# Later conversion stages, another PSUM buffer for one state part, and a new order of one projection in a linear-attention and feed-forward kernel

## The chip, the core and the metric

The kernel runs on one core of one Trainium2 chip. The metric is the device time of one execution in microseconds (us). Five engines work side by side, each through its own instructions in order: TensorE (PE, matrix products; the loading of its weights is shown apart as PEld), VectorE (DVE), ScalarE (ACT), GpSimd (POOL) and SyncE (SP, which here only issues transfers). They wait for each other through semaphores.

## What is computed

The reference has two parts. The first is a linear attention with decay, over 4 batches, 8 heads, 768 tokens and a head dimension of 48:

```python
for t in range(S):
    cur = np.einsum('bhd,bhe->bhde', u[None] * kt, vt)
    y[:, :, t] = np.einsum('bhd,bhde->bhe', rt, state + cur)
    state = wt[:, :, :, None] * state + np.einsum('bhd,bhe->bhde', kt, vt)
```

Its output, with the heads put side by side, is x: 3072 tokens by 384. The second part is a feed-forward layer with 2048 hidden columns:

```python
h = x @ w_in
sp = np.maximum(h, 0.0) + np.log1p(np.exp(-np.abs(h)))
g = h * erf(sp)
return (g @ w_out).astype(np.float32)
```

The arrays w_in and w_out are given as 64-bit floats; the kernel turns them into 32-bit floats itself, by operations on their words.

## The kernel before

**Steps.** The work is cut into twelve steps, s = 0 to 11. A step handles 128 tokens of two batches and all their heads. The code counts from zero, and so does this text: the change's title calls s = 1 "step two" and s = 2 "step three".

**The attention of a step** (`attend`, for s = 0 to 4) goes through six levels. A level makes products of r and k with each other on PE (`level_products`, L436) in a PSUM buffer `pp`; `scale` (L252, VectorE) multiplies r and k by decays for the next level, in place, so it must wait until PE has read them; `take_level` copies the masked products into `own` (L448 on VectorE for levels two to five, two copies of L455 on ScalarE for level six; level one is L651). Then PE multiplies `own` by v (L470, `from_own`, in two calls), transposes k (L663, copied to `kT` by ScalarE at L667), and makes the state part (L522, `state_part`), which VectorE adds to the state (L690 or L692, then L693 on GpSimd, then L695). Last, `through_state` (L496) adds what the old state gives; ScalarE copies the result to xT (L503 to L506), and six small transfers (L510), three issued by SP and three by ScalarE, move the rest of it into place.

**The two `pp` buffers.** `products` hands out the PSUM buffers pp0 and pp1 in turn. While the weights are being converted it always gives pp0, and pp1 belongs to the conversion. Whoever writes such a buffer waits until its last content has been read.

**The feed-forward of a step** runs later, in pieces between the attention's products. `hidden` (L731) multiplies xT by w_in: of step s - 1, a piece being two tiles of 128 hidden columns, six matmuls, and a copy to h on ScalarE (L740). There are sixteen such tiles in two groups g of eight. Softplus (L713), erf (L716) and the product with h (L720, VectorE) follow group by group. `project` (L754) multiplies the result by w_out: of step s - 3, in pieces of four matmuls, group by group and in a group first all eight tiles for output j = 0 and then for j = 1; the output is copied at L763 and stored. In step 1 the pieces are those of step 0's hidden layer, one at each place; in step 3 the first projection runs.

**The conversion of the weights** (`convert`) is cut into sixteen chunks of two tiles, 0 to 7 for w_in and 8 to 15 for w_out. A chunk has three stages: `load` (L194, 768 KB, issued by SP, three buffers), `scale` (two operations on ScalarE: L207 into pp1, L209 into `rest`) and `join` (VectorE: L216 on pp1 and L219 from pp1 to the weights; GpSimd: the add L223). Since pp1 is one buffer, a chunk's L207 waits for the L219 of the chunk before. A load waits for the L219 that frees its buffer.

**What sets the order.** All five engines take their instructions in the order in which the program writes them. `place(n)` is called after level n + 1 and at the ends of a step; in steps 0 to 3 it sends the letters of the table CONVERT (L811) to the conversion, `l`, `s` and `j` for the three stages, and then a piece of the feed-forward follows. In steps 1 and 2 the letters go ahead of the softplus and erf stages. Entry n of a row belongs to place n; entry 8 is sent behind the step's `through_state`. So chunk k's stages stand at fixed places: in step 1, place 0 joins chunk 2 and scales chunk 3, between L651 and the scaling for level two, and place 4 joins chunk 6 and scales chunk 7, ahead of level six. Piece k of step 1 reads chunk k.

Of the kernel before, what the change touches and what calls it, by code (L numbers as in the profile page):

```python
# [11 lines left out]
FP32 = mybir.dt.float32  # L12
# [3 lines left out]
ALU = mybir.AluOpType  # L16

P = 128
EP = 64
HC = 64  # L20
NC = 2
NJ = 2
FG = 8
# [18 lines left out]
LOG = 6  # L42
# [18 lines left out]
def kernel(  # L61
# [14 lines left out]
    nc = tc.nc  # L76
    PSUM = bass.MemoryType.PSUM

    n_steps, _, _, JP, C = rkw.shape
# [45 lines left out]

    turns = {"next": 0, "converting": False}

    def products(shape):


        n = 0 if turns["converting"] else turns["next"]
        turns["next"] = 1 - n
        return ps_p.tile(shape, FP32, name=f"pp{n}")
# [46 lines left out]
    def convert(weights):  # L180

        held = {}

        def load(i):
            if i >= len(weights):
                return
            dst, src = weights[i]
            if src.dtype == FP32:  # L190
                nc.sync.dma_start(out=dst, in_=src)
                return
            words = wide.tile([P, 2, DM, 2], I32, name="words", bufs=3)
            nc.sync.dma_start(  # L194
                out=words[:].rearrange("p i n two -> p i (n two)"), in_=src.bitcast(I32)
            )
            held[i] = [words]

        def scale(i):
            if i in held:  # L200
                words = held[i][0]
                low, high = words[:, :, :, 0], words[:, :, :, 1]
                base = ps_p.tile([P, 2, NP * C], FP32, name="pp1")[:, :, :DM]
                rest = wide.tile([P, 2, DM], I32, name="rest", bufs=2)


                nc.scalar.mul(out=base, in_=high.bitcast(FP32), mul=2.0**-112)  # L207

                nc.scalar.mul(out=rest[:], in_=low.bitcast(U32), mul=2.0**-29)  # L209
                held[i] += [base.bitcast(I32), rest]  # L210

        def join(i):
            if i in held:
                words, bits, rest = held.pop(i)
                into = weights[i][0].bitcast(I32)
                nc.vector.tensor_scalar(  # L216
                    out=bits, in0=bits, scalar1=3, scalar2=None, op0=ALU.logical_shift_left
                )
                nc.vector.scalar_tensor_tensor(  # L219
                    out=into, in0=words[:, :, :, 1], scalar=-(1 << 31), in1=bits,  # L220
                    op0=ALU.bitwise_and, op1=ALU.bitwise_or,
                )
                nc.gpsimd.tensor_tensor(out=into, in0=into, in1=rest[:], op=ALU.add)  # L223

        done = {"l": 0, "s": 0, "j": 0}
        for _ in range(3):
            load(done["l"])
            done["l"] += 1
        while True:
            what = yield  # L230
            {"l": load, "s": scale, "j": join}[what](done[what])
            done[what] += 1
            if weights[0][1].dtype != FP32:
                turns["converting"] = 0 < done["s"] and done["j"] < len(weights)
                turns["next"] = 0

    def rows(e, n=D):
# [372 lines left out]
    def attend(s, xT, place, behind):  # L610

        c, in_t, vt, made, S, S_next, ends = parts_of(s)
        K = in_t[:, 1]
        RK = in_t[:, 0:2]


        following = prepare(s + 1) if s + 1 < n_steps else iter(())
        own = made if s >= DIRECT else att.tile([P, NH, HC], FP32, name="own")

        def keep_busy(*columns):  # L620
            zeros = states[1][0][:].rearrange("p n d -> p (n d)")
            for n in columns if not s else ():
                nc.tensor.matmul(
                    y[:].rearrange("p e j q t -> p (e j q t)")[:, :n], lhsT=ident[:],
                    rhs=zeros[:, :n], start=True, stop=True, skip_group_check=True,
                )

        def stay_warm(times=1, where=None):
            for _ in range(times):
                ps = where or ps_m.tile([P, NP * C], FP32, name="m")  # L630
                nc.tensor.matmul(
                    ps[:], lhsT=ident[:], rhs=ws[s][:, :NP], start=True, stop=True
                )

        if s == DIRECT:
            next(following)
        for level in range(near_log(s) + 1 if s == DIRECT else 1, LOG + 1):
            rk = made[:] if level == 1 else RK
            pp = products([P, NE, JP, HC])
            level_products(pp, rk, level)  # L640
            if level == LOG and s == DIRECT:
                spread_blocks(s + 1, pp)
            scale(s, level)
            keep_busy(DM, DM // 2)
            if level == 1 and s == 1:
                stay_warm()
            got = pp[:].rearrange("p e n t -> p (e n) t")
            if level == 1:
                if not s:
                    nc.vector.tensor_copy(out=first[:], in_=mask_sb[:, 0, :])  # L650
                nc.vector.tensor_mul(  # L651
                    own[:], got, first[:, None, :].to_broadcast([P, NH, HC])
                )
            else:
                take_level(own, pp, level)
            if level > 1 and (s, level) != (DIRECT, LOG - 1):
                next(following, None)
            place(level - 1)

        from_own(s, own, 1)  # L660
        ps = products([P, JP, P])
        for n in range(JP):
            nc.tensor.transpose(ps[:, n, :], K[:, n, :], ident[:])  # L663
        if not s:
            stay_warm()
        kT = att.tile([P, NH, D], FP32, name="kT", bufs=1)
        nc.scalar.copy(  # L667
            kT[:].rearrange("p (e n) d -> p e n d", e=NE),
            ps[:].rearrange("p n (e d) -> p e n d", e=NE)[..., :D],
        )  # L670
        if c:
            nc.gpsimd.tensor_mul(
                faded[0][:], S[:], ends[:, :, 0:1].to_broadcast([P, JP, D])
            )
        next(following, None)
        place(LOG)


        if s:
            ps = products([P, NC, JP, HC])  # L680
            ps = [ps[:, h] for h in range(NC)]
        else:
            ps = [ps_m.tile([P, JP, HC], FP32, name="m") for h in range(NC)]
        state_part(s, kT, ps)
        from_own(s, own, 0)
        if not s:
            stay_warm(1, products([P, NP * C]))
        for e in range(NE):
            if c:
                nc.vector.tensor_add(middle[rows(e)], faded[0][rows(e)], ps[0][rows(e), :, :D])  # L690
            else:
                nc.vector.tensor_copy(middle[rows(e)], ps[0][rows(e), :, :D])  # L692
        nc.gpsimd.tensor_mul(faded[1][:], middle[:], ends[:, :, 1:2].to_broadcast([P, JP, D]))  # L693
        for e in range(NE):
            nc.vector.tensor_add(S_next[rows(e)], faded[1][rows(e)], ps[1][rows(e), :, :D])  # L695
        for _ in following:
            pass
        place(LOG + 1)
        through_state(s, xT)
        behind()  # L700
# [44 lines left out]
    def project(s, gs):  # L745

        c, i = divmod(s, SPC)
        ps = [None] * NJ
        for g in range(NG):
            for j in range(NJ):  # L750
                if not g:
                    ps[j] = ps_m.tile([P, DM], FP32, name="m")
                for f in range(FG):
                    nc.tensor.matmul(  # L754
                        ps[j][:],
                        lhsT=gs[g][:, f, j * C : (j + 1) * C],
                        rhs=w_out_sb[:, g * FG + f, :],
                        start=g + f == 0,
                        stop=g == NG - 1 and f == FG - 1,
                    )  # L760
                    if g == NG - 1 and f == FG - 1:
                        o = outs.tile([P, DM], FP32, name="o")
                        nc.scalar.copy(o[:], ps[j][:])  # L763
                        nc.sync.dma_start(out=out[i * NJ + j, c], in_=o[:])
                    if f % 4 == 3:
                        yield
# [29 lines left out]
    def in_order(s, k):  # L796
# [13 lines left out]

    CONVERT = (  # L811
        ("", "", "", "", "", "s", "jls", "j", "sl"),
        ("jsl", "jsl", "jsl", "jsl", "jsl", "j", "", "", "sl"),
        ("jsl", "jsl", "jsl", "jsl", "jsl", "js"),
        ("js", "j"),
    )

    STAGES = {
        1: (0, 0, 0, 0, 0, 0, 1, 0), 2: (1, 0, 0, 0, 0, 0, 1, 1), 3: (1, 2, 1, 0, 0, 2, 1, 1)
# [8 lines left out]
    with tc.manual_schedule(  # L828
# [20 lines left out]
        for s in range(n_steps):  # L849
# [31 lines left out]
            if s > DIRECT:  # L881
                attend_late(s, place)
                continue
            attend(s, xTs[s], place, lambda: convert_at(LOG + 2))
            if s + 2 < n_steps:
                load_step(s + 2)
                if s + 2 == DIRECT:
# [107 lines left out]
```

## Time and profile before

| what | value |
| --- | --- |
| median of 9 runs | 619.95 us (619.19 to 621.9) |
| the profiled execution | 620.11 us |
| its span in the profile | 618.3 us |
| PE busy | 604.4 us |
| DVE, ACT, POOL busy | 412.4, 293.5, 291.7 us |
| PE busy between 104.8 and 130.0 us | 25.20 us |
| stretch in which the steps 1 and 2 lie | about 32 to 104 us |

The profile is one execution recorded by the hardware. A line of its timeline has the start, the duration, the engine, the line of the kernel, the operation, the tiles (result, arrow, operands), their shapes and the number of instructions that were merged, and in brackets how long the engine had been idle ahead of it and what ended that. An idle engine costs time only if somebody on the chain that ends last waits for it. A wait for several semaphores is put down to the one that the profile saw last, so the name in the brackets can be that of another.

### The profile page before, as it was taken

To read this page: it belongs to the slowest core of one execution; us is meant where nothing else is said; L and a number is where in the kernel's file an instruction comes from. 1 tells how busy PE (TensorE), PEld (TensorE's weight loads), DVE (VectorE), ACT (ScalarE), POOL (GpSimd) and SP (SyncE) were. 2 spreads that over 40 slices of the span, in tenths; PEclk is the share of its full clock that TensorE was granted. 3 is DMA by queue.
4 is the path that set the end of the run, shared out by engine and by line. 5 is a ranking of instruction groups with operands and counts; after the bars stand their busy time and mean duration, and the time that the engine had idled before them with its cause. 6 is when DMAs were issued, how large, how long until landed. Compare 5 with 4: busy or idle time off the path is not lost.

```text
span 618.3 us, 15587 instructions
## 1 busy us (share of the span) xinstructions
PE 604.4 (98%) x6858; PEld 447.4 (72%) x6858; DVE 412.4 (67%) x459; ACT 293.5 (47%) x374; POOL 291.7 (47%) x295
## 2 busy tenths in 40 slices
PE   8989999999999999999999999999999999999997
PEld 7657787678668768668768768768768768668654
DVE  5688598795995897897797797797797311110300
ACT  2537878725536634443443543543543443634600
POOL 4349274602497389299189299299297000000000
PEclk9899999999999999999999999999999999999999
DMA  8276381531333305415415415414402200000000
GB/s 325 102 285 210 131 268 53 206 138 19 136 98 116 121 28 174 124 37 176 104 55 178 120 38 177 119 39 142 124 33 67 36 26 1 9 25 1 0 27 25
DMA packets 51371, 63.27 MB, mean 102 GB/s; under 512 B 34920, under 2 KB 40296, under 8 KB 49896
## 3 DMA queue, kind: packets, MB, share of 16 engines
q1 hardware_dynamic: 50152, 61.68, 31.2%
q8 instruction: 54, 0.88, 0.6%
q10 hardware_dynamic: 1152, 0.59, 0.4%
q14 instruction: 13, 0.11, 0.1%
HBM read 52.39 MB, written 8.69 MB: 99 GB/s over the span
## 4 chain that ended last, share of the span: by engine, by line
PE 86%; DVE 6%; DMA 3%; issue 2%; ACT 1%; POOL 1%; SPq 0%; POOLq 0%; ACTq 0%; DVEq 0%
PE m L754 38%; PE m L731 37%; PE pp L436 5%; DMA w<-in_rkw 3%; PE y L470 2%; PE pp L522 1%; PE y L496 1%; DVE in L252 1%; PE pp L663 1%; DVE sums L356 1%; DVE pp L216 1%; DVE words L370 1%; DVE own L448 1%; POOL tot_sb L304 1%; DVE w_in_sb L219 0%
## 5 line engine op out<-in xcount | busy, mean ns | idle before, releaser
L731 PE MATMUL m<-xT,w_in_sb 128*128 128x256 f32 x1152 | 257.2, 382 | 1.4 <-DVE w_in_sb L219 1.2
L754 PE MATMUL m<-w_out_sb,h 128*128 128x384 f32 x768 | 252.2, 488 | 0.0
L731 PEld LDWEIGHTS m<-xT,w_in_sb 128*128 128x128 f32 x1152 | 216.1, 190 | 33.7 <-issue 2.8
L754 PEld LDWEIGHTS m<-w_out_sb,h 128*128 128x128 f32 x768 | 144.5, 190 | 98.6 <-POOL w_out_sb L223 0.4
L740 ACT COPY h<-m 128x512 f32<-128x512 f32 x96 | 55.9, 582 | 128.3 <-PE m L731 128.2
L720 DVE TENSOR_TENSOR h<-h,sp 128x1024 f32<-128x1024 f32 x48 | 76.0, 1623 | 52.0 <-ACT sp L716 51.8
L252 DVE TENSOR_TENSOR in<-in,tot_sb 128x1024 f32<-128x1024 f32 (+1 forms) x60 | 86.0, 1441 | 30.4 <-PE pp L436 28.0
L370 POOL TENSOR_TENSOR words<-words,rest 128x528 f32<-128x528 f32 (+10 forms) x77 | 85.5, 1111 | 6.0
L366 POOL TENSOR_TENSOR rk<-words 128x528 f32<-128x528 f32 (+3 forms) x28 | 44.5, 1590 | 82.5 <-DVE sums L356 72.1
L763 ACT COPY o<-m 128x384 f32<-128x384 f32 x24 | 11.5, 480 | 110.3 <-PE m L754 110.3
L304 POOL TENSOR_TENSOR tot_sb<-tot_sb 128x256 f32<-128x256 f32 (+4 forms) x60 | 53.8, 896 | 4.5
L436 PEld LDWEIGHTS pp<-in 48*64 48x64 f32 (+1 forms) x2368 | 34.1, 127 | 16.8 <-issue 9.7
L716 ACT ACTIVATE sp<-sp 128x2048 f32<-128x2048 f32 x24 | 45.9, 1911 | 0.3
L713 ACT ACTIVATE sp<-h 128x2048 f32<-128x2048 f32 x24 | 45.9, 1911 | 0.3
L436 PE MATMUL pp<-in 48*64 48x64 f32 (+1 forms) x2368 | 38.6, 214 | 4.2 <-DVE in L252 1.5
L356 DVE TENSOR_REDUCE sums<-words 128x6 f32<-128x288 f32 (+8 forms) x66 | 29.2, 469 | 19.2 <-POOL words L366 19.0
L716 ACT ACT_TABLE_LOAD x24 | 30.8, 1283 | 16.6 <-issue 11.3
L366 POOL TENSOR_TENSOR words<-words 128x336 f32<-128x336 f32 (+6 forms) x49 | 35.0, 715 | 3.8
L356 DVE TENSOR_REDUCE sums<-rk 128x14 f32<-128x672 f32 (+9 forms) x54 | 34.8, 703 | 0.2
L713 ACT ACT_TABLE_LOAD x24 | 30.8, 1283 | 4.6 <-issue 4.2
L370 DVE TENSOR_TENSOR words<-words,rest 128x576 f32<-128x576 f32 (+8 forms) x34 | 26.4, 776 | 1.2
L223 POOL TENSOR_TENSOR w_out_sb<-w_out_sb,rest 128x768 int32<-128x768 int32 x8 | 18.1, 2262 | 18.4 <-DVE w_out_sb L219 18.3
(80 smaller groups left out, 441.4 us busy)
## 6 DMA issues: line engine op xcount, KB each, us to landing
in<-in_rkw SPq DMA_DIRECT2D x11, 1024.0 KB, 5.3
words<-in_moe_w_in SPq DMA_DIRECT2D x8, 768.0 KB, 4.5
words<-in_moe_w_out SPq DMA_DIRECT2D x8, 768.0 KB, 5.8
words<-in_rk_rows SPq DMA_DIRECT2D x8, 768.0 KB, 6.6
w<-in_rkw SPq DMA_DIRECT2D x11, 512.0 KB, 8.2
v<-in_v SPq DMA_DIRECT2D x12, 384.0 KB, 5.8
out<-o SPq DMA_DIRECT2D x24, 192.0 KB, 2.0
rest<-in_w_rows SPq DMA_DIRECT2D x8, 384.0 KB, 8.0
```

Source lines behind the costliest of these rows:

```text
L252: nc.vector.tensor_mul(halves, halves, view(tots[level - 1], 0, [[1, n], [2, nb], [0, half]]))
L304: nc.gpsimd.tensor_mul(new, pair[:, :, 0], pair[:, :, 1])
L356: nc.vector.tensor_reduce(out=view(sums[:], n, [[near * (NEAR + 1), NEAR // near], [NEAR + 1, near - n]]), in_=terms[n], axis=mybir.AxisLi ...
L366: engine.tensor_mul(terms[n], r[:, :, n:], k[:, :, : near - n])
L370: engine.tensor_mul(k[:, :, :m], k[:, :, :m], w[:, :, n : n + m])
L436: nc.tensor.matmul(pp[s0 : s0 + m, e, n, :m], lhsT=rk[rows(e), 1, n, s0 : s0 + m], rhs=rk[rows(e), 0, n, t0 : t0 + m], start=True, stop=True,)
L713: nc.scalar.activation(held[0][:], h[:], AF.Softplus)
L716: nc.scalar.activation(held[0][:], held[0][:], AF.Erf)
L720: nc.vector.tensor_mul(h[:, part], h[:, part], held[0][:, part])
L731: nc.tensor.matmul(ps[:, ff, :], lhsT=w_in_sb[:, g * FG + f + ff, kk * P : (kk + 1) * P], rhs=xT[:, kk, :], start=kk == 0, stop=kk == KT - 1,)
L740: nc.scalar.copy(h[:, f : f + FT, :], ps[:])
L754: nc.tensor.matmul(ps[j][:], lhsT=gs[g][:, f, j * C : (j + 1) * C], rhs=w_out_sb[:, g * FG + f, :], start=g + f == 0, stop=g == NG - 1 and ...
```

## The change

Four things are changed.

First, `join` is split: its first VectorE operation (L216) becomes a stage of its own, `shift` ("h"), and the rest is stage "o"; the letter "j" still sends both, one after the other.

Second, the table of stages for the steps 1 and 2 is rewritten. In step 1, place 0 sends only the shift of chunk 2 and a load; the rest of that join and the scaling of chunk 3 are sent in level two, between `scale` and `take_level` (BEHIND_SCALING). In both steps place 4 no longer scales a chunk; that scaling comes at place 5, behind the copies of `own` of level six, ahead of the join there. In step 2 the scaling that stood at place 5 moves to place 6, behind the copy of kT.

Third, in step 1 the state part goes to pp1 instead of pp0.

Fourth, in the projection of step 0, the second group of tiles is taken in another order: tiles 8 to 11 for both outputs, then tiles 12 to 15 for both.

The number of instructions of each kind stays the same.

```diff
-    def products(shape):
+    def products(shape, n=None):
+        if n is not None:
+            return ps_p.tile(shape, FP32, name=f"pp{n}")
         n = 0 if turns["converting"] else turns["next"]
...
+        def shift(i):
+            if i in held:
+                bits = held[i][1]
+                nc.vector.tensor_scalar(
+                    out=bits, in0=bits, scalar1=3, scalar2=None, op0=ALU.logical_shift_left
+                )
+
         def join(i):
             if i in held:
                 words, bits, rest = held.pop(i)
                 into = weights[i][0].bitcast(I32)
-                nc.vector.tensor_scalar(
-                    out=bits, in0=bits, scalar1=3, scalar2=None, op0=ALU.logical_shift_left
-                )
...
+        stages = {"l": load, "s": scale, "h": shift, "o": join}
...
-            {"l": load, "s": scale, "j": join}[what](done[what])
-            done[what] += 1
+            for stage in {"j": "ho"}.get(what, what):
+                stages[stage](done[stage])
+                done[stage] += 1
...
             if level == 1 and s == 1:
                 stay_warm()
+            if s == 1 and level == 2:
+                behind(None)
...
-            ps = products([P, NC, JP, HC])
+            ps = products([P, NC, JP, HC], 1 if s == 1 else None)
...
+        halves = [slice(0, FG // 2), slice(FG // 2, FG)]
         for g in range(NG):
-            for j in range(NJ):
-                if not g:
+            for j, part in (
+                [(j, part) for part in halves for j in range(NJ)]
+                if not s and g == NG - 1
+                else [(j, part) for j in range(NJ) for part in halves]
+            ):
+                if not g and not part.start:
...
-                for f in range(FG):
+                for f in range(FG)[part]:
...
         ("", "", "", "", "", "s", "jls", "j", "sl"),
-        ("jsl", "jsl", "jsl", "jsl", "jsl", "j", "", "", "sl"),
-        ("jsl", "jsl", "jsl", "jsl", "jsl", "js"),
+        ("hl", "jsl", "jsl", "jsl", "jl", "sj", "", "", "sl"),
+        ("jsl", "jsl", "jsl", "jsl", "jl", "sj", "s"),
         ("js", "j"),
...
+    BEHIND_SCALING = "os"
...
-            attend(s, xTs[s], place, lambda: convert_at(LOG + 2))
+            def behind(n=0):
+                if n is not None:
+                    convert_at(LOG + 2)
+                    return
+                for what in BEHIND_SCALING:
+                    conversion.send(what)
+
+            attend(s, xTs[s], place, behind)
```

## The prediction

> **What bounds the kernel now.** First the page's busy times and its chain.
>
> ```profile
> span 618.3 us, 15587 instructions
> PE 604.4 (98%) x6858; PEld 447.4 (72%) x6858; DVE 412.4 (67%) x459; ACT 293.5 (47%) x374; POOL 291.7 (47%) x295
> PE 86%; DVE 6%; DMA 3%; issue 2%; ACT 1%; POOL 1%; SPq 0%; POOLq 0%; ACTq 0%; DVEq 0%
> ```
>
> TensorE (PE) is busy 98% of the span and makes 86% of the chain. The change takes no matmul away, so it can win only what PE idles. PE's waits between 30 and 110 us, where all edits but one lie (us in total, times, longest):
>
> ```profile
> PE pp L436 <- DVE own L448: 1.4, 2, 1.2
> PE m L731 <- DVE w_in_sb L219: 1.2, 1, 1.2
> PE pp L436 <- DVE s L695: 0.9, 1, 0.9
> PE y L470 <- ACT own L455: 0.8, 3, 0.3
> ```
>
> That is 4.3 us. The second wait (at 35.69) lies ahead of every edit and stays. From 104.8 to 130 us PE was busy 25.20 of 25.20 us, and after that only two gaps stand (0.34 and 1.07 us), so what PE gains before step 3 should reach the end. Times below are those of this profile, "old" where a gain has already shifted them; steps count from 0.
>
> **A. Step 1, level two: chunk 2's join goes behind the scaling.** The timeline there (start, us):
>
> ```profile
> 39.88 1.82 POOL L223 TENSOR_TENSOR w_in_sb<-w_in_sb,rest 128x768 int32<-128x768 int32 x1 [1.46 <-DVE w_in_sb L219]
> 40.16 2.62 DVE L252 TENSOR_TENSOR in<-in,tot_sb 128x1024 f32<-128x1024 f32 x1 [0.43 <-PE pp L436]
> 42.70 1.28 DVE L448 COPY_PREDICATED own<-mask_sb,pp 128x512 f32<-128x512 int32 x1
> ...
> 44.13 1.16 PE L436 MATMUL pp<-in 48*64 48x64 f32 x64 [1.25 <-DVE own L448]
> ```
>
> VectorE's scaling (L252) took 2.62 us beside GpSimd's add (L223), against 1.22 in the next level (at 45.74): it stood until the add ended at 41.70. PE then waited 1.25 us for L448, which empties pp0. In the changed order L219 of chunk 2, which releases that add, comes after L252. From start to start: L252 to its successor 1.14 (45.74 to 46.88), L219 to its successor 0.87 (48.48 to 49.35), L448 to PE 1.43 (42.70 to 44.13). PE's level three starts at 40.16 + 1.14 + 0.87 + 1.43 = 43.60, a gain of 0.53. The other 0.72 stay, because L219 still stands ahead of L448. Bounds: 0 and the whole 1.25.
>
> What becomes late: chunk 2's add starts at 42.3 and ends at 44.2 (1.82 alone); PE needs it at 44.69. Stretched to 2.68 as at 45.97, it would cost PE 0.3. ScalarE's scaling of chunk 3 waits for that L219 (pp1): L207 at 42.3, 0.87 long, done as VectorE reaches L216 at 43.26. The h copy that stood behind it (41.38) goes ahead. SP's load of chunk 5 waits for L219 too: issued at 42.3, not 39.80, with the two loads behind it. Chunk 5 is read at 49.47 old, 48.94 new: 6.6 us of room. Loads of this size landed in 4.2 to 10.9 us, the longest ones in the queue behind step loads; here the step loads left SP by 38.7, so I take 4.5 and no cost.
>
> The Trainium skill ("SBUF — State Buffer", section "The DMA setup-cost knee") puts a transfer at about 2 us and its bytes at 436 GB/s, 3.8 us for this load as an estimate. By that the later load could never be felt; by the row of 10.9 us it would be, and the sum would turn (rival 4).
>
> **B. Step 1, last level: chunk 7's scaling goes behind the copies of own.**
>
> ```profile
> 56.87 0.88 ACT L207 ACTIVATE pp<-words 128x768 f32<-128x768 f32 x1 [1.30 <-DVE w_in_sb L219]
> 57.68 0.90 ACT L209 ACTIVATE rest<-words 128x768 int32<-128x768 uint32 x1
> 58.48 0.57 ACT L740 COPY h<-m 128x512 f32<-128x512 f32 x1
> 58.95 1.17 ACT L455 COPY own<-pp 32x512 f32<-32x512 f32 x2
> ...
> 60.17 0.65 PE L470 MATMUL y<-own,v 64*48 64x64 f32 x28 [0.28 <-ACT own L455]
> ```
>
> PE's level six ends at 56.53, but L455 runs at 58.95, behind L207, L209 and an h copy; L470 therefore ends at 60.76 (where L663 starts), not 0.58 after piece five (59.51 + 0.58 = 60.09). New order: h copy, L455 at 56.6 to 57.8, then L207 and L209 to 59.5, all before PE's piece five ends. Gain 0.67. Piece five itself waits for an add ending at 56.59, which moves with A. Nothing else takes the place: the kT copy idled 1.15 for L663 already, and chunk 7's join ends about 60.6 (L207 to 58.65, L216 and L219 0.95 each), its add by 62.4, needed at 65. Bounds: 0 (if ScalarE is late again) to 0.75.
>
> **C. Step 1's state part in pp1.** This takes away PE's wait for L695 at 68.73: 0.89 us. I count it as nothing. Behind these products PE has three matmuls that are ready, then six that need xT, in order:
>
> ```profile
> 68.97 1.79 SPq L510 DMA_DIRECT2D xT<-y  x3
> ...
> 71.83 0.30 PEld L731 LDWEIGHTS m<-xT,w_in_sb 128*128 128x128 f32 x2 [0.42 <-issue]
> ...
> 72.46 0.73 PEld L731 LDWEIGHTS m<-xT,w_in_sb 128*128 128x128 f32 x4 [0.33 <-issue]
> ```
>
> The weight loads at 71.83 and 72.46 stand by the same distances from the issue (2.86, 3.49) as in the step before (36.31 and 37.01, issued 33.49: 2.82, 3.52). So the third xT transfer paces PE already, and four matmuls follow it whatever came before. xT hangs on ScalarE's copies after L496, which C leaves alone. PE will wait for xT where it waited for L695. Bounds: 0 and 0.89. The added waits are slack: L522 needs pp1 at 64.4, free since 60.6; chunk 8's L207 needs L695 (68.58) and started at 71.20, behind the DMA issues.
>
> **D. Step 2, last level, the same move as B.** L455 at 93.34 stands behind L207/L209 (91.25) and an h copy; L663 starts at 95.14. New: L455 at 90.95, so L470 follows piece five (start of L470 at 93.63, plus 0.58): L663 at 94.21, gain 0.93. Then the vector side is late:
>
> ```profile
> 97.67 1.82 POOL L672 TENSOR_TENSOR faded<-s,tot_sb 128x384 f32<-128x384 f32 x1
> ...
> 99.83 1.14 DVE L690 TENSOR_TENSOR middle<-faded,pp 48x384 f32<-48x384 f32 x2 [1.03 <-PE pp L522]
> ```
>
> Chunk 13's join now ends at 94.9 (L455 to 92.1, L207 to 93.0, then 0.95 twice), later than 94.27. Its add (1.8 alone), two L720 (4.60 beside two adds; 2.35 for two at 142.14) and L672 (1.82 here; the same shape took 0.83 at 101.11) stand in each other's way, as A's scaling and add did: 94.9 + 1.2 + 1.7 + 1.1 + 0.8 = 99.7. L690 starts there, not at 99.83; L695 ends 3.27 later (as old) at 102.95; PE's first level of step 3, whose pp0 this state part still fills, starts 0.15 after that (68.58 to 68.73): 103.1 instead of 103.79. Gain 0.7 of the 0.93. Bounds: 0.2 and 0.93. Chunk 14's scaling now precedes an h copy and the softplus: ScalarE reaches L503 at 103.75, old 104.04, and xT is not needed until 130.
>
> **E. Tiles 12 to 15 last.** The add of the last chunk ended at 121.59 and held a weight load 0.39 us, but PE had no gap. New, those tiles start after another level, at 124.2. Counted as 0; bounds 0 and 0.4. Output j = 0 leaves one piece later, and nothing waits for it: hid(2)'s first piece needs its bank at 130.7, after the copy.
>
> **Sum.** 0.53 + 0.67 + 0 + 0.7 + 0 = 1.9. The profiled execution took 620.11 (span 618.3 and 1.8 around it): 618.2. It lies 0.16 over the median of nine, so against 619.95 I expect **618.0**.
>
> **Rivals.**
> 1. C pays. If xT came early enough, 0.89 more: 617.1. Against it: the two weight loads above. Chance 0.1.
> 2. D is eaten: L690's chain on VectorE and GpSimd decides, and A's add meets VectorE. A + B less 0.2: 1.0 us, 619.0. For it: pp0 is kept in step 2, and L672 stands behind one more add. Chance 0.2.
> 3. The change doesn't do what it says: VectorE or ScalarE is late by as much elsewhere in the same level. Within 0.5 of before: 619.9. Chance 0.12.
> 4. Slower, by chunk 5's later load. Over 8.0 us to landing (6.6 of room, 0.76 that VectorE runs ahead, 0.6 that PE's level six gives), each further us is one of PE. At 10.9 that is 2.9 less the 1.9 won: 620.9; it loses from 9.9 us on. Against it: 0.4 MB at most is ahead of it, and the load issued at 35.63 landed in 4.2. Chance 0.06.
>
> The forecast has the remaining 0.52, from 617.5 to 618.7. What a measurement of this kernel can tell from no change is about 0.2%, 1.24 us, so the line lies at 618.7. Faster: 0.5 of the forecast, rival 1 and a little of rival 2, 0.63. Same: 0.31, from the rest of rival 2, rival 3 and part of rival 4. Slower: 0.06, the tail of rivals 3 and 4. The range leaves out rival 4 and half of rival 3 above, and the lower edge of rival 1: 616.9 to 619.8.
>
> **What would show it.** A: PE's wait before step 1's level three 0.7, and L252 about 1.2 long. B and D: no wait of PE for L455 in steps 1 and 2. C: products right behind L496 in step 2, then PE waiting about 1 us for xT before L731. D: a PE wait near 0.2 for L695 before step 3. E: no weight load held by L223. Wrong: a wait for words or ScalarE's L207 near 49 us, or PE's gain at the end of step 3 differing from that at the end.

## The result, and the profile after

The changed kernel takes 617.5 us (median of 10 runs, 617.38 to 618.79); the kernel before, on the same chip, takes 620.79 (31 runs, 619.07 to 622.71). The ratio is 0.9952, with a 95% interval of 0.994 to 0.9964: 3.3 us faster, against a forecast of 1.9. The sign and the range hold, and 617.5 lies 0.5 below the forecast of 618.0. That is closer than the gain was forecast: the median of the kernel before came out 0.84 us higher with 31 runs than the 619.95 of nine that the forecast started from, and the gain 1.4 us larger. One term of the sum was mis-sized, and below it is found.

The profiled execution took 617.53 us. First the lines of the page that answer to those shown of before: span, busy times and the engines' shares of the chain that ended last.

```profile
span 615.7 us, 15592 instructions
PE 602.0 (98%) x6858; PEld 446.2 (72%) x6858; DVE 409.4 (66%) x459; ACT 293.8 (48%) x374; POOL 293.7 (48%) x295
PE 86%; DVE 7%; issue 2%; POOL 2%; ACT 2%; DMA 1%; SPq 0%; DVEq 0%; ACTq 0%; POOLq 0%
```

PE still makes 86% of the chain. Its busy time fell by 2.4 us with the same 6858 matmuls: part of what the profile of before showed as busy was slow PE, and that comes back below. PE's waits between 34 and 110 us (us in total, times, longest), the view that carried the prediction (the lines of the changed kernel have numbers up to 17 higher):

```profile
PE m L742 <- DVE w_in_sb L225: 1.2, 1, 1.2
PE m L742 <- DMA xT<-y: 1.0, 1, 1.0
PE pp L444 <- DVE own L456: 0.9, 2, 0.8
```

Of the four waits of before, the one for L455 (now L463) is gone, the one for `own` of level two went from 1.2 to 0.8, and the one for s L695 has turned into one for xT of about the same size (0.9 and 1.0). In the timeline, A stands as forecast: the scaling L260 takes 1.23 us where it took 2.62, because the add of chunk 2 (L229) is now released behind it, and PE's wait before level three is 0.77 (start, us, engine, line, tiles, and in brackets the idle time ahead and what ended it):

```profile
39.15 1.23 DVE L260 TENSOR_TENSOR in<-in,tot_sb 128x1024 f32<-128x1024 f32 x1 [1.41 <-PE pp L444]
40.29 0.95 DVE L225 SCALAR_TENSOR_TENSOR w_in_sb<-words,pp 128x768 int32<-128x768 int32 x1
41.15 1.33 DVE L456 COPY_PREDICATED own<-mask_sb,pp 128x512 f32<-128x512 int32 x1
...
41.38 1.83 POOL L229 TENSOR_TENSOR w_in_sb<-w_in_sb,rest 128x768 int32<-128x768 int32 x1 [3.97 <-DVE w_in_sb L225]
...
42.63 1.16 PE L444 MATMUL pp<-in 48*64 48x64 f32 x64 [0.77 <-DVE own L456]
```

B in the same view: the copies of `own` run at 55.07, ahead of chunk 7's scaling, and PE's L478 follows its piece without a gap.

```profile
55.07 1.18 ACT L463 COPY own<-pp 32x512 f32<-32x512 f32 x2
...
56.15 0.87 ACT L209 ACTIVATE pp<-words 128x768 f32<-128x768 f32 x1
57.04 0.93 ACT L211 ACTIVATE rest<-words 128x768 int32<-128x768 uint32 x1
...
57.95 0.66 PE L478 MATMUL y<-own,v 64*48 64x64 f32 x32
```

C: the first products of step 2 now start right behind L504 (they overlap it in the record), and PE then idles 0.99 us for xT. The wait has changed its name and not its size.

```profile
64.97 0.66 PE L504 MATMUL y<-in,middle 48*48 48x64 f32 x32
65.45 1.11 PE L444 MATMUL pp<-rk 48*64 48x64 f32 x64
66.49 1.56 PE L742 MATMUL m<-xT,w_in_sb 128*128 128x256 f32 x6
69.05 3.13 PE L742 MATMUL m<-xT,w_in_sb 128*128 128x256 f32 x12 [0.99 <-DMA xT<-y]
```

**Where the 2.6 us between the two profiled executions come from.** I read the start of the first products of steps 1, 2, 3 and 4 on PE in both. Before: 32.30, 68.73, 103.79, 156.53, end 618.3; after: 31.29, 65.45, 100.68, 153.43, end 615.7. So 1.0 us is won before step 1, where nothing was changed; 2.1 us in steps 1 and 2; nothing between steps 3 and 4; and 0.5 is lost again behind step 4. The prediction named as a sign of being wrong that the gain at the end of step 3 differs from that at the end: it is 3.1 us there (156.53 less 153.43) and 2.6 at the end. The first and the last amount need an explanation that is not the change.

The first one: the granted clock. Windows of the profile of before (busy time with the number of instructions for PE, PEld, DVE, ACT, POOL, then the granted clock, the DMA share and GB/s) show 0.61 and 0.53 at 16 to 20 us; the profile after has 1.00 there.

```profile
14.00:16.00 2.00, 0.76 (x50) 0.63 (x45) 0.99 (x1) 0.00 (x0) 0.00 (x0) 1.00 1.01 416
...
16.00:18.00 2.00, 2.00 (x21) 1.33 (x22) 1.38 (x2) 0.00 (x0) 0.00 (x0) 0.61 0.98 398
18.00:20.00 2.00, 2.00 (x55) 1.56 (x57) 0.46 (x1) 1.21 (x4) 0.00 (x0) 0.53 0.55 212
```

The same four matmuls of step 0 (L623 before, L631 after; at 16.45 and 16.57) took 2.29 us there and 1.24 after. It is a property of one execution: of the ten runs of the changed kernel, three have a mean clock of 0.997 and take 618.3 to 618.8, and seven have 1.00 and take 617.4 to 617.6. So this 1.0 us is not won by the change, and there must be something else in the medians. The experiments look for it.

### The profile page after: what moved, and what is told of

It is laid out like the page before. It is cut to its first block, busy times and chain, and to the rows that moved or that the text cites. A ratio compares the mean times of both kernels' runs of the same rounds, so it can differ in the third digit from the quotient of the medians.

```text
span 615.7 us, 15592 instructions
## 1 busy us (share of the span) xinstructions
PE 602.0 (98%) x6858; PEld 446.2 (72%) x6858; DVE 409.4 (66%) x459; ACT 293.8 (48%) x374; POOL 293.7 (48%) x295
## 4 chain that ended last, share of the span: by engine, by line
PE 86%; DVE 7%; issue 2%; POOL 2%; ACT 2%; DMA 1%; SPq 0%; DVEq 0%; ACTq 0%; POOLq 0%
PE m L771 38%; PE m L742 37%; PE pp L444 5%; DVE in L260 2%; PE y L478 2%; PE y L504 1%; PE pp L530 1%; POOL w_in_sb L229 1%; DMA in<-in_rkw 1%; DVE w_in_sb L225 1%; PE pp L673 1%; DVE sums L364 1%; DVE pp L217 1%; DVE own L456 1%; DVE words L378 1%
## 5 line engine op out<-in xcount | busy, mean ns | idle before, releaser
L771 PE MATMUL m<-w_out_sb,h 128*128 128x384 f32 x768 | 252.1, 488 | 0.0
L771 PEld LDWEIGHTS m<-w_out_sb,h 128*128 128x128 f32 x768 | 144.8, 190 | 98.3
L751 ACT COPY h<-m 128x512 f32<-128x512 f32 x96 | 55.8, 582 | 130.6 <-PE m L742 130.5
L731 DVE TENSOR_TENSOR h<-h,sp 128x1024 f32<-128x1024 f32 x48 | 74.6, 1594 | 52.3 <-ACT sp L727 52.1
L260 DVE TENSOR_TENSOR in<-in,tot_sb 128x1024 f32<-128x1024 f32 (+1 forms) x60 | 84.6, 1418 | 30.2 <-PE pp L444 28.5
L312 POOL TENSOR_TENSOR tot_sb<-tot_sb 128x256 f32<-128x256 f32 (+4 forms) x60 | 53.0, 883 | 4.5
L727 ACT ACTIVATE sp<-sp 128x2048 f32<-128x2048 f32 x24 | 45.9, 1911 | 0.3
L444 PEld LDWEIGHTS pp<-in 48*64 48x64 f32 (+1 forms) x2368 | 33.8, 126 | 16.4 <-issue 8.4
L444 PE MATMUL pp<-in 48*64 48x64 f32 (+1 forms) x2368 | 38.4, 212 | 3.8 <-DVE in L260 1.5
L378 DVE TENSOR_TENSOR words<-words,rest 128x576 f32<-128x576 f32 (+8 forms) x34 | 27.9, 819 | 1.2
L229 POOL TENSOR_TENSOR w_out_sb<-w_out_sb,rest 128x768 int32<-128x768 int32 x8 | 17.8, 2220 | 17.8 <-DVE w_out_sb L225 17.7
```

The source lines that it names most:

```text
L260: nc.vector.tensor_mul(halves, halves, view(tots[level - 1], 0, [[1, n], [2, nb], [0, half]]))
L312: nc.gpsimd.tensor_mul(new, pair[:, :, 0], pair[:, :, 1])
L378: engine.tensor_mul(k[:, :, :m], k[:, :, :m], w[:, :, n : n + m])
L444: nc.tensor.matmul(pp[s0 : s0 + m, e, n, :m], lhsT=rk[rows(e), 1, n, s0 : s0 + m], rhs=rk[rows(e), 0, n, t0 : t0 + m], start=True, stop=True,)
L727: nc.scalar.activation(held[0][:], held[0][:], AF.Erf)
L731: nc.vector.tensor_mul(h[:, part], h[:, part], held[0][:, part])
```

## The experiments

The theory after the result: A, B and D do what the prediction says, C is covered, and E is worth nothing or little. The rival: a part counted as nothing (C or E) pays, and the profiled execution of before hid it. Each part was run alone and, for C and E, left out of the whole; then one part was moved further, and one piece put off. For each run I give the time beside the kernel before on the same chip, and the stretches between landmarks of the profile, since a stretch is measured to some hundredths and a median of these runs only to about 0.7 us.

| kernel | median, us | before, us | ratio, 95% interval | step 1 to 3 | step 3 to 4 |
| --- | --- | --- | --- | --- | --- |
| before, profiled first | | | | 71.49 | 52.74 |
| after | 617.5 | 620.79 | 0.9952 (0.994 to 0.9964) | 69.39 | 52.75 |
| before again | 620.75 | 620.57 | 1.0006 (0.9989 to 1.0023) | 71.49 | 54.30 |
| A alone | 620.09 | 620.57 | 0.9993 (0.9981 to 1.0004) | 71.00 | 54.30 |
| B alone | 620.03 | 620.57 | 0.9993 (0.9981 to 1.0005) | 70.86 | 54.29 |
| D alone | 619.54 | 620.57 | 0.9984 (0.9971 to 0.9997) | 70.70 | 54.34 |
| C alone | 620.24 | 620.34 | 0.9998 (0.9988 to 1.0008) | 71.46 | 54.30 |
| all but C | 618.43 | 620.34 | 0.9975 (0.9963 to 0.9986) | 69.47 | 52.75 |
| all but E | 618.55 | 620.34 | 0.9972 (0.9954 to 0.9991) | 69.41 | 54.35 |
| join behind the copy too | 617.85 | 620.34 | 0.9968 (0.9953 to 0.9983) | 70.38 | 52.75 |
| E alone | 620.46 | 620.66 | 0.9997 (0.9986 to 1.0008) | 71.49 | 52.71 |
| piece put off | 620.55 | 620.66 | 0.9999 (0.9984 to 1.0015) | 73.60 | 52.75 |
| put off, early scaling | 619.7 | 620.66 | 0.9996 (0.9978 to 1.0014) | 75.19 | 52.75 |
| the same without C | 621.21 | 620.66 | 1.0011 (0.9994 to 1.0028) | 71.21 | 52.76 |

The stretches are in us, from the start of one step's first products on PE to that of another.

**The kernel before, once more.** No edit.

> The kernel before, unchanged, once more, to see how much of the 2.6 us between the two spans is not the change. In the profile before, step 0's fifth level began at 22.18 us and step 1's first level at 32.30, in the one after at 20.59 and 31.29: 1.0 us ahead of every edit. Theory 1 (the granted TensorE clock, 0.61 and 0.53 in two stretches between 16 and 20 us of the profile before, 1.00 after): it comes and goes with the execution, so runs of this kernel fall into a group at about 619.1 us with a mean clock of 1.00 and one about 1.2 to 1.7 us higher with 0.996 to 0.997, and a profile without the dip has step 1's first level near 31.3. Rival: the change itself moved the start; then every run of this kernel has step 1's first level near 32.3 and a clock below 1.00. In either case the distance from step 1's first products to step 3's first products stays at 71.5 us (103.79 less 32.30).

Its profile has a mean clock of 1.000 and starts step 1 at 31.21, about where the changed kernel does (31.29), so the late start of 32.30 belongs to the first profile and not to the kernel. Still its span is 619.3 us, 1.0 more than that of the first profile. The expected grouping by clock did not come: its six runs with a mean clock of 1.000 spread from 619.17 to 621.46, so something else differs between executions too. From step 3 to step 4 it needs 54.30 us instead of 52.74: 1.56 us more, where the undisturbed start saves 1.09. The place, on PE, in the first projection:

```profile
116.65 4.14 PE L754 MATMUL m<-w_out_sb,h 128*128 128x384 f32 x12
122.11 1.56 PE L754 MATMUL m<-w_out_sb,h 128*128 128x384 f32 x4 [1.32 <-POOL w_out_sb L223]
```

PE waits 1.32 us for the add of the last chunk, the one that E gives more time. So the first profile of before hid what E is for. What differs is on GpSimd. In this run:

```profile
112.91 2.98 POOL L304 TENSOR_TENSOR tot_sb<-w 128x512 f32<-128x512 f32 x1 [3.98 <-DMA w<-in_rkw]
115.97 3.71 POOL L304 TENSOR_TENSOR tot_sb<-tot_sb 128x256 f32<-128x256 f32 x5
119.64 2.41 POOL L223 TENSOR_TENSOR w_out_sb<-w_out_sb,rest 128x768 int32<-128x768 int32 x1
...
112.62 2.35 DVE L720 TENSOR_TENSOR h<-h,sp 128x1024 f32<-128x1024 f32 x2
```

And in the first profile of before:

```profile
114.07 1.76 POOL L304 TENSOR_TENSOR tot_sb<-w 128x512 f32<-128x512 f32 x1 [4.06 <-DMA w<-in_rkw]
115.90 2.94 POOL L304 TENSOR_TENSOR tot_sb<-tot_sb 128x256 f32<-128x256 f32 x5
118.93 2.66 POOL L223 TENSOR_TENSOR w_out_sb<-w_out_sb,rest 128x768 int32<-128x768 int32 x1
...
117.73 5.47 PE L754 MATMUL m<-w_out_sb,h 128*128 128x384 f32 x16
...
113.68 3.22 DVE L720 TENSOR_TENSOR h<-h,sp 128x1024 f32<-128x1024 f32 x2
```

GpSimd's product of 128x512 meets two products of VectorE (L720) that stand one behind the other. Either VectorE keeps the way for both (2.35 for the two, and L304 takes 2.98), or GpSimd gets in between (L304 1.76, the two L720 3.22). In the first case the five products behind it meet other VectorE work too (3.71 instead of 2.94), and the add ends at 122.05. PE wanted it at 120.62: it is for the thirteenth matmul of the block, the twelfth started at 120.30, and they follow each other by 0.32. In the second case the add ended at 121.59 and the thirteenth started on time, at 121.70; the weight load behind the add came so late that the block took 5.47 us where the others take 5.43. Measured from the first products of step 1 the add ends at 90.84 against 89.29, 1.55 us later, and with next to no room in the second case that is the 1.56 by which the stretch grows. The Trainium skill ("SBUF — State Buffer", section "SBUF: two separate sides") says that the two engines share one pair of ports and that whoever starts first has it for a whole instruction while the other blocks. The rows agree, but it doesn't tell who is next when VectorE has a second instruction ready: of the 14 profiled executions of this case VectorE kept it in twelve (L304, or L312, of 2.47 to 3.07 us), and in two GpSimd got it (1.76 and 1.68). The offset between the two starts doesn't decide: 0.39 us in the first profile of before, 0.43 in the profile after, with opposite outcomes; with A alone and with E alone it is 0.46 in both, again with opposite outcomes.

**A alone, B alone, D alone.** Cores of the edits, in the tables of stages:

```diff
-        ("jsl", "jsl", "jsl", "jsl", "jsl", "j", "", "", "sl"),
+        ("hl", "jsl", "jsl", "jsl", "jsl", "j", "", "", "sl"),
```
```diff
-        ("jsl", "jsl", "jsl", "jsl", "jsl", "j", "", "", "sl"),
+        ("jsl", "jsl", "jsl", "jsl", "jl", "sj", "", "", "sl"),
```
```diff
-        ("jsl", "jsl", "jsl", "jsl", "jsl", "js"),
+        ("jsl", "jsl", "jsl", "jsl", "jl", "sj", "s"),
```

> Only edit A: in step 1 the join of chunk 2 and the scaling of chunk 3 go behind the scaling of level two; the rest as before. Measured from step 1's first products to step 3's first products (before 71.49 us, after 69.39). Theory: A is worth the 0.5 us that the wait ahead of level three loses (1.25 to 0.77), so 71.0, and the waits for own in steps 1 and 2 stay. Rival: the port that L252 and the add share was not the reason, and A only moves work: 71.5, or worse if ScalarE's scaling of chunk 3 is now late.

> Only edit B: in step 1 chunk 7's scaling goes behind the copies of own; the rest as before. From step 1's first products to step 3's first products (before 71.49 us). Theory: 0.7 us less, 70.8, with no wait of TensorE for L455's copies in step 1 and 0.55 still there in step 2. Rival: B pays only together with A, because piece five waits for an add of GpSimd: then below 0.3, 71.2 or more.

> Only edit D: in step 2 the scalings of chunks 13 and 14 go back by one place each; the rest as before. From step 1's first products to step 3's first products (before 71.49 us). Theory: 0.8 us less, 70.7, of 0.93 that the two late copies of own cost; the rest is a wait for L695 ahead of step 3's first level, under 0.15 us. Rival (the prediction's second): VectorE and GpSimd at the end of step 2 eat it, 0.2 to 0.5 less, 71.0 to 71.3.

From step 1 to step 3 they save 0.49, 0.63 and 0.79 us (71.49 less 71.00, 70.86 and 70.70). The prediction had 0.53, 0.67 and 0.7. Together 1.91, of the 2.10 that all parts save there. In the medians A and B lie within the interval around no change, D just beyond it.

**C alone, and all but C.**

```diff
-            ps = products([P, NC, JP, HC], 1 if s == 1 else None)
+            ps = products([P, NC, JP, HC])
```

> Only edit C: step 1's state part goes to the other PSUM buffer; the rest as before. From step 1's first products to step 3's first products (before 71.49 us). Theory: nothing, 71.4 to 71.5: the wait of 0.89 us for L695 goes and TensorE waits about 1 us for xT, some two microseconds later. Rival: C gives its 0.89, 70.6.

> The changed kernel without edit C. From step 1's first products to step 3's first products (after 69.39 us). Theory: the same within 0.1, 69.4, with the wait of 0.9 us for L695 back ahead of step 2's first level and the one for xT gone. Rival: without it 0.9 are lost, 70.3.

C alone saves 0.03 us between the landmarks, and leaving it out of the whole costs 0.08. The pair of waits swaps as forecast: C alone has 1.0 for xT and none for L706, all but C has 0.9 for L706 and none for xT. The median of all but C stands 0.9 us above that of the changed kernel, and by the ratios to the runs of before beside each it is 1.4 (0.9975 less 0.9952, of 620). Its profile has no such loss between the landmarks, but 0.9 more in waits named "issue" in front of or within L504 behind 155 us (2.5 against 1.6 in all). I put it down to these; that is not shown, and neither is that C has a part in them.

**All but E.**

```diff
-                if not s and g == NG - 1
+                if False
```

> The changed kernel with the first projection's tiles in the old order (edit E undone). From step 1's first products to step 4's first products, which lie behind all of step 3. Theory: the same within 0.1 us as the changed kernel, because the add of the last chunk ends just when its tiles are due; a weight load may wait for it by 0.3 to 0.6 us without a gap on TensorE. Rival: now that TensorE comes 2 us earlier the add is late, and TensorE waits 0.3 to 1 us for it in the first projection.

The expected "same within 0.1 us" didn't come, and its rival did, larger than its 0.3 to 1 us. The stall is there again: L771 waits 1.33 us for L229, and step 3 to step 4 takes 54.35 us. In the whole, leaving E out costs 1.60 us of that stretch. The profiled execution also shows a granted clock of 0.50 from 18 to 24 us, and its step 1 starts at 33.35. So here both come together, the low clock and the stall; the first doesn't prevent the second.

**Join behind the copy too.** A, moved one instruction further: chunk 2's join behind `take_level` as well, to win the remaining 0.77.

```diff
-            if s == 1 and level == 2:
-                behind(None)
...
                 take_level(own, pp, level)
+            if s == 1 and level == 2:
+                behind(None)
```

> The changed kernel, with the join of chunk 2 and the scaling of chunk 3 sent behind the copy L448 of level two instead of ahead of it. Level three then needs no more than the scaling and the copy, so the 0.77 us that TensorE still waits there go. From step 1's first products to step 3's first products (after 69.39 us). Theory: the chunk's add ends 1.1 us later, near 44.3 of the changed profile, while its tiles are due at 43.0; TensorE waits there about 1.4 us instead: 70.0, a loss of 0.6. Rival: the add has room, the whole wait is won: 68.6.

The wait for L456 in level two is gone, and a larger one takes its place: chunk 2's add now ends at 44.05, and PE waits 1.46 us for it ahead of 44.10, and 0.4 in a second wait for such an add (rows of PE's waits from 34 to 110 us):

```profile
PE m L742 <- POOL w_in_sb L229: 1.9, 2, 1.5
PE m L742 <- DVE w_in_sb L225: 1.2, 1, 1.2
PE m L742 <- DMA xT<-y: 1.0, 1, 1.0
```

It costs 0.99 us against the changed kernel (70.38 less 69.39), where 0.6 was expected. The place between the scaling and the copy is the right one: the next instruction over, the join is already too late.

**E alone.** Everything as before but the order of the tiles.

> The kernel before with part E alone: in the second group of step 0's projection tiles 12 to 15 come last, and nothing else is changed. Theory now, after the run without E: the add of the last chunk (GpSimd) ends at about 122 when the kernel's start is not disturbed, and PE waits 1.3 to 1.5 us for it; E takes that wait away. So from step 3's first products to step 4's PE needs 52.75 us instead of 54.30, from step 1's first products to step 3's still 71.49, and the median is 1.5 us below the kernel before: ratio 0.9975. Rival, which is what the prediction had: E is covered, the stretch from step 3 to step 4 is the same in both but for what the profile of one execution happens to show, ratio 1.000.

The stretch is 52.71, as expected, but this execution can't prove it: GpSimd got in between here (L312 1.68), so the add would have been in time in the old order too. The proof is in the changed kernel, all but C, and four more: there VectorE kept the way, the add ended as late as in the stalled ones, and the stretch is still 52.75. The expected ratio of 0.9975 didn't come: 0.9997, with an interval that excludes it. The profiled execution, the slowest of the twelve runs (622.28), stands still for 2.8 us behind step 4 in two waits named "issue", more than any other, and the second wait is followed by a low clock:

```profile
439.83 0.37 PE L504 MATMUL y<-in,s 48*48 48x64 f32 x10 [1.50 <-issue]
...
440.63 9.70 PE L771 MATMUL m<-w_out_sb,h 128*128 128x384 f32 x24
```

```profile
440.00:442.00 2.00, 2.00 (x46) 1.45 (x41) 1.97 (x3) 1.20 (x4) 0.00 (x0) 0.75 0.04 8
442.00:444.00 2.00, 2.00 (x4) 1.07 (x4) 1.90 (x4) 0.21 (x1) 0.00 (x0) 0.50 0.12 33
444.00:446.00 2.00, 2.00 (x7) 1.04 (x6) 1.93 (x3) 1.99 (x2) 0.00 (x0) 0.89 0.64 156
```

This wait is 0.42 in the profile after, at the same place, with nothing visible that PE waits for. So by the profiles E is worth 1.55 us in an execution in which VectorE keeps the way, and nothing in one in which GpSimd gets in; by the medians it is worth about 0.2 us alone (620.66 less 620.46, within the interval) and 1.2 in the whole (0.9972 less 0.9952, of 620; the two intervals overlap). Single runs agree with the first part: E alone needs 619.66 to 620.61 in its seven runs with a mean clock of 1.000, the kernel before on that chip 619.20 to 621.37 in twenty. So with E alone the upper end is gone; but if E only took a stall away, its runs should lie at the lower end, and they lie about 1 us above it. A rival is left: what E wins in step 3 may be lost in part behind step 4. From step 4's first products to the end of the span the seven profiled executions without E need 461.5 to 462.3 us, the seven with E 461.5 to 465.1, the excess in pauses like the one above and in the low clock. Nothing was run to tell this from chance, and how often VectorE keeps the way in the runs that weren't profiled stays open too.

**The first piece of step 2 put off.** The changed kernel, with one more edit, to see whether xT is the only cover of C, and whether the 0.99 us at 69 us can be had:

```diff
-            kind, of, pieces = hids, s - 1, 1
+            kind, of, pieces = hids, s - 1, {(2, 0): 0, (2, 1): 2}.get((s, k), 1)
```

> The changed kernel, and in step 2 the first piece of the hidden layer, whose six matmuls need the late xT, is put off behind level two, where it comes together with the second one. If the wait for xT is all that covers part C, PE's wait of 0.99 us at 69 us goes, and from step 1's first products to step 3's it takes 68.4 instead of 69.39. Theory: there is a second cover behind it. Level two writes pp0, which VectorE's L661 reads (66 to 69 us: L706, L260 and L661 one after the other, 1.2 each), so PE waits until 69.0 for L661 instead: 69.3, a gain of 0.1 at most, and the line of PE's wait names own L661 in place of xT.

The second cover is there: PE waits 0.88 us for own L661 where it waited for xT. The size was missed by far, 73.60 instead of 69.3, because a third wait appears that I had not thought of. Two pieces in one place fill PSUM tiles that ScalarE empties (h, L751), and their copies stand behind an activation and a conversion (L727, L209 and L211, up to 77.95):

```profile
68.61 1.16 PE L444 MATMUL pp<-in 48*64 48x64 f32 x64 [0.88 <-DVE own L661]
69.70 5.45 PE L742 MATMUL m<-xT,w_in_sb 128*128 128x256 f32 x24
75.08 1.16 PE L444 MATMUL pp<-in 48*64 48x64 f32 x64
78.57 4.29 PE L742 MATMUL m<-xT,w_in_sb 128*128 128x256 f32 x12 [2.33 <-ACT h L751]
82.79 1.35 PE L444 MATMUL pp<-in 48*64 48x64 f32 x64
```

The twelve at 78.57 took 4.29 us and those of the next levels 2.86: from 80 to 82 us the granted clock was 0.50, from 82 to 84 it was 0.69. So a wait of 2.33 us cost 1.4 more behind it.

**Put off, with an early scaling; and the same without C.** Both have the edit of the run before. VectorE's scaling for step 2's first level goes ahead of step 1's copies of `middle`, which frees L661 from the queue of three. The second of the two kernels also takes C back (`products([P, NC, JP, HC], None)`).

```diff
         place(LOG)
+        if s == 1:
+            scale(2, 1)
...
-            scale(s, level)
+            if (s, level) != (2, 1):
+                scale(s, level)
```

> As the run before, and VectorE scales r and k for level one of step 2 ahead of the two copies of middle in step 1 (it idles 4 us there; the scaling needs r and k, which ScalarE has read by 62.2). Now L661 can start at 66.7 and end at 67.9, so both covers of part C are gone: level two follows at 68.1 and xT is there when its matmuls come. Theory: from step 1's first products to step 3's 68.45 instead of 69.39 in the changed kernel, and 0.9 us less in all: the fastest of all, near 616.6. Rival: a third thing holds PE there (the scaling for level three, behind the join of chunk 8), and the gain is below 0.3.

> As the run before, but without part C: step 1's state part stays in pp0. Step 2's first level then waits for VectorE's L706 (to 66.7), ends at 67.8, L661 at 69.1, and level two starts at 69.2. Theory: C, worth 0.03 to 0.08 us in the kernels so far, is worth about 1.0 here: from step 1's first products to step 3's 69.4. Rival: C is worth nothing here either, 68.45.

Neither of my numbers came. Level two does follow without a gap in the first (68.00 + 1.56, then 69.49), so both covers are off at that place. But the matmuls behind level two then wait 1.38 us for xT, and the copies of h hold PE for 1.62 us again, with a granted clock of 0.50 at 82 to 84 us. Without C, PE waits 1.11 us ahead of the first products (the profile names ACT xT L513; L709, which frees pp0, ended at 66.68, just ahead of PE's 66.82), and in step 2 never for xT. From the start of L504 to the end of the two pieces the first takes 77.60 - 66.47 = 11.13 us and the second 75.90 - 65.05 = 10.85, which looks as if C were worth nothing here either. But the xT transfers of that step took 3.3 us from issue to landing in the first, and 1.8 to 1.9 in the other thirteen profiled executions. Had they landed 1.4 us earlier, the wait of 1.38 would be gone and the first would take about 9.75, an estimate from these rows: 1.1 less than without C, near the 1.0 that was expected. The medians point the same way (619.7 with C, 621.21 without), within intervals that overlap. So what C is worth here stays open, and the run doesn't show that xT would pace this place in general. The difference of 4 us between the two from step 1 to step 3 is not C: the first lost 1.4 ahead of L504 (a wait "issue" of 1.03 at 52.47 among it), and 2.3 behind level three, in the low clock and a wait of 0.92 for `own`. Nor are the two executions typical: the first is the slowest of its twelve runs (624.99), the second among the fastest of its own (619.66). No version tried is better than the changed kernel.

## Why the prediction was right, and where it was not

- **A: right.** 0.53 forecast, 0.49 measured alone and in the whole (from step 1's first products to level three 11.83 us before and 11.34 after); a wait of 0.7 forecast, 0.77 seen; L260 at 1.23. Sound because each interval came from a row of the same operations without the neighbour.
- **B: right.** 0.67 forecast; 0.63 alone.
- **C: right as a sum and as a mechanism.** 0 forecast, 0.03 and 0.08 measured; the wait for xT came at 0.99. The weight loads that stood at the same distance from the issue of xT in two steps were the evidence, and they held. The vector side would have been a second cover: with the first piece put off PE waited 0.88 us for L661.
- **D: right.** 0.7 of 0.93 forecast, 0.79 alone. L701 starts 5.33 us after PE's transposes, 5.49 forecast; the small wait for L706 ahead of step 3 did not show.
- **Rival 4** (chunk 5's later load) never came up: issued at 41.30, and its reader at 47.99 waited for VectorE's L225 and not for the transfer.
- **E: the step that failed, in size.** "The add of the last chunk ended at 121.59 and held a weight load 0.39 us, but PE had no gap", and therefore 0 with an upper bound of 0.4. The profiled executions show 1.55 us in place of it, in each of those without E but that first one (step 3 to step 4 in 54.29 to 54.35 us, and 52.71 to 52.76 with E). How much of it reaches the end is less sure: by the medians 1.2 in the whole and 0.2 alone. My evidence was that PE was busy 25.20 of 25.20 us. That was true of one execution, and the margin in it was 121.70 less 121.59, 0.11 us; the held weight load, which the prediction saw, was the sign of it. A row that ends 0.11 us ahead of its reader on an engine that shares a port is not cover; the two L720 ahead of it took 3.22 there and 2.35 at 142.14 in the same profile, a row that the prediction itself used for D. That should have been read as one outcome of two, and the upper bound set by the other: where VectorE kept the way, the add came 1.55 us later.
- **The base.** The execution that I summed against carried 1.0 us of a low clock at its start, and lacked the stall of 1.55. The two nearly cancel, so its time lay near the median, and I took that for a sign that it was typical. That the forecast still came out within 0.5 us is in part luck: its gain was 1.4 us short, and its base 0.84 us low. Of undisturbed executions the kernel before needs 71.49 + 54.30 from step 1 to step 4 and the changed one 69.39 + 52.75: 3.65 us less. The medians say 3.3.

## What to carry to other kernels

A gap of nothing in one profile is a statement about one execution: look at how far ahead of its reader the last writer ended, and if that is a few tenths on an engine that shares something with a neighbour, price the other outcome too. Before a sum is made against a profiled execution, compare its granted clock slice by slice with 1.00, since a disturbance that costs and a stall that happens to be absent can add up to the median. When work is moved from one late place, the next later place is often already too late (0.99 us lost by one instruction in the join, 4.2 us by one piece of the hidden layer, 1.4 of it by a low clock), so check each reader behind the new place, PSUM tiles included.

## What the runs showed of the hardware

- **PE's clock falls after some pauses of PE between 1.2 and 2.3 us, and not after most.** It went to about 0.5 after pauses of 1.24 (before, at 15.97), 1.50 (E alone, and all but E near 16 us), 2.33 (the first put-off kernel), and 1.62 and 1.61 us (put off with the early scaling, at 80.39 and 257.41). It stayed at 1.00 after 1.33 (after, at 16.09), 1.49 and 1.98 (put off without C), and after some thirty other pauses of 1.2 to 1.5 us. How busy PE was just before doesn't decide: 0.76 of 2.00 us ahead of the drop shown above, 0.75 in the same slice of the profile after, without a drop. Over its slices the clock that is missing adds up to 1.7 us each time (0.39 and 0.47 of 2 us in the profile of before; 0.25, 0.50 and 0.11 with E alone), and to 3.4 in the run of all but E: at a clock of 0.5 that is a stretch of 3.4 us, and once of 6.8, as an estimate. The Trainium skill ("TensorE: Matmul & The Clock Gate", section "What's actually happening") has the clock halve after an idle window of about 3.4 us that runs freely; that the same pause counts once and not another time would fit a free-running window, but the pauses here are shorter than the window, so by these measurements 1.24 us can be enough.
- **Pauses without a visible cause.** Ahead of, or within, a block of L504 or L444 PE stood still for 0.2 to 1.6 us with nothing that the profile shows as a reason ("issue"), at places that most executions share (near 253 and 440 us), with sizes that differ: 1.23 and 0.42 after, 1.25 and 1.50 with E alone. They may make much of the scatter of these runs; that, and their cause, is not shown.
- **Who gets between two instructions of VectorE is not fixed.** Twelve times VectorE kept the way for both and GpSimd's product took 2.47 to 3.07 us instead of 1.68 and 1.76; twice GpSimd got in, and VectorE's two took 3.22 instead of 2.35 to 2.40.
- **A small transfer can land late for once.** The xT transfers of 16 KB in step 1 landed 1.8 to 1.9 us after their issue in thirteen profiled executions, and 3.3 us after it in one (put off with the early scaling). Nothing here shows why.
